# RWKV7 attention with a GELU MLP on one core: four heads of the attention's output stay in the tile in which they are made, the fifth column alone passes DRAM, and the first 430 entries of the order are new

## The chip, the cores and the metric

The kernel runs on one core of a Trainium2 chip. The core has five engines that run side by side: TensorE (PE, matmuls), VectorE (DVE), ScalarE (ACT), GpSimd (POOL) and SyncE (SP), which here does nothing but issue DMAs. The metric is the time of one execution on the device in microseconds (us); several executions are made and the median is taken.

## The reference

```python
def _attn_ref(r, k, v, w, a, b):                 # (4, 8, 768, 40) each: batch, heads, seq, head_dim
    state = np.zeros((B, H, D, D), dtype=np.float32)
    for t in range(S):
        y[:, :, t] = np.einsum('bhd,bhde->bhe', rt, state)
        Sa = np.einsum('bhde,bhe->bhd', state, at)
        state_decay = state * wt[:, :, None, :] - np.einsum('bhd,bhe->bhde', Sa, bt)
        state = state_decay + np.einsum('bhd,bhe->bhde', vt, kt)

def _moe_ref(x, w_in, w_out):                    # (3072, 320), (320, 2048), (2048, 320)
    h = x @ w_in
    g = h * (1.0 / (1.0 + np.exp(-1.702 * h)))
    return (g @ w_out).astype(np.float32)

x = np.ascontiguousarray(attn_out.transpose(0, 2, 1, 3)).reshape(B * S, H * D)
return _moe_ref(x=x, **moe_kwargs)
```

A recurrence over 768 time steps for each batch and head, and then an MLP over all 3072 tokens. All is computed in float32.

## The kernel before

**Units.** Time is cut into 12 chunks `c` of 64 steps, the batches into 2 pairs `p`. A unit is `i = 2c + p`. Inside a chunk the recurrence is turned into matrix products: decays are summed (`ps_cum`, `ps_cumc`), ScalarE takes their exponentials (`G`, `GT`, `FT`), inputs are scaled by them (`b`, `ak`, `rv`, `kh`, `bh`), a triangular 64x64 matrix `N` is made for each head and inverted in five levels (`ps_level`), right sides `B0` and `B1` are built (`ps_B`), solved (`ps_X`, `M`), and one last group of matmuls (`ps_y`, `read`) gives both the output of the chunk and the state for the next. From `ps_y`, `updated` makes the new state, `read_out` the sum of output terms, and `decayed` (L956 to L962) multiplies by the decay and so makes x, the attention's output, of the unit, with 40 channels of a head on the partitions of one half (rows 0 to 39 and 64 to 103) and heads and time along the free axis.

**The MLP** of a chunk follows both of its units. It needs x with all 320 channels along the contraction, as 5 columns `k` of 64 rows in each half (`xT`, three slots, so three chunks). Before, x goes through DRAM for that: `part_with` (L967) writes the tile x, 80 KB from each half, to a DRAM tile of 320 rows, and `get_back` (L973) reads it into both halves of `xT`, 160 KB each. An `up` task (L986) is 4 matmuls (two instructions each) for one of 4 quarters `q` of the hidden size, one `m` of 2 and one `k` of 5: 40 tasks a chunk. `gelu` (L995) is one ScalarE instruction per `q`. `down` has 8 parts for each `p`, and then two evictions and a store.

**Weights.** The 8 pieces of w_in and w_out come in four quarters each, as pairs of words, and pass four instructions (L447, L455, L459, L463) before they can be used. Their raw data lies in places that are free at the start; that of the fifth piece lies in slots 1 and 2 of `xT`, so those slots may be written only once this piece is joined.

**Order.** All work is 2700 tasks, each with the tasks that it must follow. A list, `ORDER`, names every task by number, the letter of its engine (p, a, d, g, s for PE, ScalarE, VectorE, GpSimd, SyncE) and the PSUM bank, and `Plan.listed` (L89) hands them out in that sequence: each engine runs its own entries in the order of the list, and waits where a task that it must follow is not done. SyncE issues its DMAs in this order too, with at most 8 in flight. A helper records every matmul, so all of PE's rows name line 300; they are told apart by tile.

```python
x_of = lambda: buf("x", i, [128, 4, 2, 64])
...
for e in BITS:
    nc.sync.dma_start(rows()[e], x_of()[64 * e:64 * e + D].rearrange("p j b t -> p (j b t)"))
```

Of the kernel before, what the change touches and what calls it, by code (L numbers as in the profile page):

```python
# [107 lines left out]
0s 5s 7s 8s 9s 3a 6s 87p0 88p1 24s 89a1 1s 2s 12s 102a 95d 100p2 90a0 93d 158a 101d2 98p3 96g 10s 94d 17s 97g 16s 99d3 103p1  # L108
4a 11s 132p0 104a1 105d1 142p2 26s 143p3 133a0 106d 130p1 14s 144a3 13s 107p0 15s 18s 151g 108a0 109d0 51s 131a1 110p3 27s
149g 150d 111a3 112d3 159p0 156p1 145a2 161d0 160a0 152g 113p3 345s 92a 162d 25s 153d 114a3 163p2 42s 115d3 34s 19a 274s 264p0  # L110
165d2 265p3 164a2 22d 266a3 166p2 20d 273s 21d 33s 43s 167a2 154p3 168d2 23g 35s 28a 157d1 116p2 155d3 169p1 117a2 118d2 267a0
279d 63s 280g 119p3 277s 171d1 36s 44s 120d3 343s 125d3 278g 124d3 29d 126p2 170a1 123a3 30d 172p1 122a3 127a2 121a 31d 128p2
54s 173a1 287a 288p0 289a0 129d2 32g 174d1 134p3 147s 37a 290d0 175p2 135d3 180a2 146s 178a2 275s 176d2 136p1 179a2 479s 38d
181a2 45s 39d 177a 282g 291d 91s 138a1 182p0 188p3 281d 183a0 186p2 139d 137a1 283p0 187a2 184p1 189a3 40d 276s 292p2 46a
284d0 41g 285p3 185d1 344s 148a 286d3 190p0 293a2 294d2 334p1 335p3 357a 140s 191d0 268g 336a3 315d 192p2 47d 337a1 348d 316p0
194a2 295p3 349d 61s 317a0 195g 60s 347s 358p1 296a3 62s 297d3 360d1 318a0 298p3 271a 361d 319p0 338g 300d3 196s 193a2 320a0
346s 355p2 385d 270s 48d 299a3 362p0 356d2 351g 301p3 363a0 364d0 350g 269s 141s 386p2 197s 302d3 365p0 387a2 352g 359a1 303d3
388a2 323p1 367d0 366a0 321p3 49d 324a1 304p2 322a3 478s 325d1 50g 353p0 309a2 470p3 354d0 209p1 307a2 210p1 310a2 305d2 211p1
308a2 272d 198p0 341a 199p0 72s 212p1 70s 64a 200p0 340s 368p2 52s 342d 339s 69s 201p0 369a2 202p0 370d2 203p0 471a 213p1 65d
214p1 389p2 66d 472a3 483g 204p0 390a2 560s 371p3 67d 306a 53s 215p1 71s 482s 216p1 372a3 217p1 476a 220p2 373d3 68g 218p1  # L120
221p2 477d 219a1 205p0 222p2 206p0 223p2 224p2 207p0 55a 311p3 225p2 79s 312d3 80s 226p2 208a0 58d 313p1 374p3 314d1 227p2 56d
379a3 228p2 229p2 57d 326p0 230a2 59g 393p1 327d0 378a3 391p2 394a1 375d3 231p0 558s 392d2 376a 232p0 233p0 395d1 559s 81s 73a
78s 234p0 480s 381p2 235p0 328p1 481s 382a2 74d 377a3 485d 380a3 236p0 75d 492a 242p2 486d 243p2 82a 76d 484d 77g 383p3 237p0
384d3 244p2 329d1 330d1 488p3 473d 238p0 531d 245p2 487g 246p2 489d3 85d 532p1 239p0 533a1 396p3 331d 332s 474s 475s 534a1
240p0 247p2 397d3 562s 241a0 535p1 83d 490p3 536a1 84d 398p0 572a 491d3 86g 550p1 555s 561s 253p3 399d0 551a 333s 400d0 254p3
401d 402s 554s 255p3 552a1 564d 493p0 705s 556a 567g 570p1 403s 494d0 248p2 563d 566g 249p2 495d0 498d 256p3 571d1 565g 250a2
496a0 251d2 252s 696p1 497g 557d 539p0 537p2 704s 257p3 538a2 540d0 258p3 553d 611d 697a 499d 573p2 784s 700s 259p3 576a2
574d2 710d 260p3 541d0 575d2 404p0 578d 261a3 577g 405p0 579d 698a1 568p2 711g 500p1 406p0 569d2 501a1 407p0 262d3 263s 708s
580p2 702a 502d1 408p0 582d2 409p0 503d 410p0 583d 504a 612p3 411p0 584g 613d3 412p0 614d3 413p0 505p1 709d 414a0 426p3 506d1
427p3 428p3 507d1 429p3 699d 581d2 430p3 615p1 785s 706s 701s 703d 431p3 616a1 585p0 432p3 508d 586a0 433p3 587d0 434p3 509a  # L130
588d 435p3 589d 448p2 436a3 510p1 590p0 511a1 449p2 592d0 591a0 512d1 415p3 513d 416p3 593d 514a 417p3 594g 418p3 515p0 419p3
516a0 517d0 595p1 518d 420p3 596a1 597d1 421p3 598d 422p3 519a 599d 423p3 424p3 520p0 425a3 437p1 521d0 438p1 523d0 522g 439p1
524d0 440p1 525d0 441p1 442p1 526d0 527p3 718p0 929s 528a3 443p1 719d0 787s 444p1 720d0 529p3 445p1 721d0 446p1 530d3 600p0
723d 447a1 542p3 722d 724g 603d0 605a0 619p1 604d0 543d3 450p2 620a1 606d0 544p3 621d1 601d0 602d 617p1 707s 546d3 451p2 618a1
783s 712d 547g 713d 607p0 725p1 608a0 452p2 609p0 453p2 548s 610d0 932s 454p2 727d1 726d1 622p0 728d 545d3 729a 775p1 455p2
623d0 780s 776a 549s 756d 730p3 624p0 456d2 457d2 731d3 458s 459p2 777a1 778g 732d3 786s 788g 781a 779s 626d0 460p2 625d0 627g
733d 795p1 835d 734a 461p2 735p3 791g 462p2 628s 736a3 796d1 737d3 716p0 792g 738d 463p2 782d 739g 1011s 920p1 757p3 925s
464p2 717d0 758a3 629s 759a3 790d 465p2 740p0 789d 466p2 741a0 742d0 921a 797p3 467d2 760p0 1008s 468d2 800a3 923d 652p2 469s
761d0 922a1 653p2 926a 930s 798d3 714p1 799d3 654p2 924s 802d 801g 655p2 934d 803a 656p2 836p0 657p2 715d1 658p2 659p2 837d0
762p3 838d0 927d 660p2 763a3 661p2 764p1 662a2 743d 630p0 744d 928s 631p0 632p0 765d1 804p3 766d1 633p0 805a3 806d3 634p0 807d  # L140
635p0 808a 745p2 636p0 748d2 637p0 749d2 839p1 933g 750d2 638p0 840a1 1009s 751d2 639p0 809p3 746d2 935g 640a0 641p1 810d3
642p1 793p2 747a 811d3 674p0 812d 794d2 813a 752p3 643p1 753a3 814p2 644p1 815a2 816d2 754p3 645p1 755d3 646p1 817d 647p1 818a
767p2 841p3 768d2 648p1 842a3 649p1 819p2 650p1 820a2 821d2 675p0 769p3 822d 651a1 823d 771d3 931s 770d3 772g 824p2 936d 676p0
827a2 828a2 942p1 829a2 677p0 1153s 830a2 937d 945a1 773s 663p3 825d2 664p3 943d1 1156s 826a 665p3 944d1 999p2 947d 946g 666p3
1000a 1004s 980d 940p1 948g 667p3 941d1 668p3 774s 669p3 670p3 831p1 671p3 1001a2 1002d 1003s 832d1 672p3 1005a 1013d 678p0
673a3 1006d 833p2 843p1 679p0 834d2 1007s 844d1 938p2 845d1 680p0 939d2 846p3 681p0 847d3 949p1 1012g 682d0 848p2 950a1 683d0
1014d 684s 685p3 849d2 1015g 1010s 850d2 1021p0 1016g 951d1 686p3 1024a0 1232s 851d 1235s 981p2 687p3 982a2 952d 852s 1022d0
983a2 953g 1144p1 1023d0 688p3 1026d 1145a 1149s 1025d 1027g 984p2 1059d 689p3 1154s 954p0 853s 985a2 1147g 690p3 1158d 1148s
955a0 956d0 986p2 1146a1 957d 1150a 691p3 958d 987a2 1151d 988p0 692p3 989a0 1152s 990d0 959p1 693a3 865p2 960a1 694d3 866p2
961d1 867p2 695s 962d 868p2 963d 1028p0 869p2 1029a0 1030d0 870p2 1031d 1157g 871p2 1159d 1032a 1060p3 872p2 873p2 1061a3  # L150
874p2 1062d3 1033p1 875a2 854p0 1035d1 855p0 1036d 856p0 1037d 1063p3 857p0 1064d3 1034a1 858p0 964p2 859p0 965a2 966d2 1038p1
967d 860p0 1039a1 1040d1 861p0 1041d 1017p3 968a 1042g 862p0 1018d3 863p0 969p2 864a0 876p1 970d2 877p1 972d2 971g 1043p3
973d2 878p1 1044a3 974d2 879p1 975d2 880p1 881p1 1045d3 1019p0 1046d 976p2 1047a 882p1 1020d0 1233s 883p1 977a2 1166p3 884p1
1169a3 1167d3 1377s 978p0 885p1 1168d3 898p2 1171d 1170g 886a1 979d0 887p3 1172a 1048p0 991p1 1051a0 888p3 1052a0 992d1 889p3
1053a0 890p3 1054a0 891p3 1049d0 993p1 1050a 1067p0 994d1 1160g 1155s 892p3 1161d 1068a0 893p3 894p3 1069d0 1380s 895p3 1204d
1065p0 995d1 896p3 996d 1066a0 1231s 1055p1 899p2 897a3 1056d1 997s 1173p0 1223p3 900p2 1174a0 1175d0 1228s 1176d 1224a 1177g
1057p1 901p2 1058d1 1070p0 998s 1164p1 1225a3 1226d 1236g 1227s 1071d0 902p2 1229a 1165d1 1162p3 903p2 1238d 1163d3 904p2
1237d 1178p0 1230d 905p2 1179a0 1180d0 1245p1 906a2 1181d 1072p3 1248a1 1456s 907d2 1182g 1246d1 908s 1247d1 909p0 1250d 1234s
1239g 1073d3 1251a 910p0 1240g 1074d3 1249d 1183p2 1459s 1283d 1368p1 911p0 1184a2 1075d 1373s 912p0 1185d2 1369a 1076s 1186d
1252p3 1187d 913p0 1370a1 1371g 1372s 1382d 1253a3 1188p2 1254d3 1374a 914p0 1255d 1190d2 1256g 1077s 1189a2 1191d 1243p1  # L160
1375d 915p0 1192g 1257p3 916p0 1244d1 1258a3 1259d3 1205p2 917d0 1206a2 1193p1 918d0 1207a2 1089p3 1260d 919s 1196a1 1090p3
# [87 lines left out]
def rwkv7_gelu_quick(ctx: ExitStack, tc: tile.TileContext, time_d, v_d, w_d, wc_d, ak_d, b_d, rv_d, w_in, w_out, out):  # L249
# [8 lines left out]
    NM = NF // 2  # L258
    NK = DM // 64
    NQ = NM // 2  # L260
    LEVELS = 5
# [721 lines left out]
    def mlp(c):  # L983
# [154 lines left out]
```

## Time and profile before

| | before |
|---|---|
| median of 3 runs | 678.64 us (678.22 to 679.32) |
| span of the profiled execution | 676.5 us |
| what lies around the span, against the median | 2.1 us |
| TensorE busy | 648.5 us, 96% |
| VectorE busy | 444.6 us, 66% |
| ScalarE busy | 331.6 us, 49% |
| GpSimd busy | 175.3 us, 26% |
| moved by DMA | 69.74 MB, 103 GB/s over the span |

The profile is one execution. The page gives busy times of engines and the span in 40 slices with one digit for each (9 is 90% or more). From the trace behind it come rows by stretch of time (windows), the chain of waits that ended last, and the timeline of each engine, in which a row may join several instructions (x4). "issue" means that the engine waited for nothing that the profile shows. A releaser such as `<-DMA b<-in_b` is what ended the idle time before an instruction.

### The profile page before, as it was taken

The page shows a single profiled execution, that of the slowest core. Times are in us where ns is not written, and L with a number is a line of the kernel's source. Part 1 is how long each engine was busy: PE and PEld are TensorE (multiplying, and loading weights), DVE is VectorE, ACT ScalarE, POOL GpSimd, SP SyncE. Part 2 cuts the span into 40 slices and gives each one's busy share as a digit, 9 for nine tenths or more (in the row PEclk, how much of TensorE's full clock was granted, in tenths as well). Part 3 has the DMA queues.
Part 4 walks back from the last instruction along what each step waited for, and adds up shares of the span by engine and source line. Part 5 has one row for each costly group of instructions (what it writes and reads, how often), then busy time and mean ns, then how long its engine had stood idle before and what let it go on. Part 6 is the DMA issues. An engine that isn't in the chain of part 4 may idle for free.

```text
span 676.5 us, 42217 instructions
## 1 busy us (share of the span) xinstructions
PE 648.5 (96%) x19488; PEld 553.4 (82%) x19488; DVE 444.6 (66%) x908; ACT 331.6 (49%) x710; POOL 175.3 (26%) x204
## 2 busy tenths in 40 slices
PE   5768999999999999999999999999999999999997
PEld 5657887987998987788888888798888798798785
DVE  4786787777867667767776587768656766675001
ACT  4676755534564655664545445455454354252110
POOL 6344244224123123123123211322412421300000
PEclk9899999999999999999999999999999999999999
DMA  7983736315314314432404413513412411200200
GB/s 230 300 289 94 232 107 187 103 43 154 108 47 149 93 58 117 121 108 72 118 22 132 141 34 109 156 33 108 140 39 71 122 53 54 61 14 15 61 12 20
DMA packets 35313, 69.74 MB, mean 103 GB/s; under 512 B 5440, under 2 KB 14656, under 8 KB 35136
## 3 DMA queue, kind: packets, MB, share of 16 engines
q1 hardware_dynamic: 35136, 67.03, 32.6%
q8 instruction: 153, 2.51, 1.5%
q14 instruction: 24, 0.20, 0.1%
HBM read 59.15 MB, written 7.86 MB: 99 GB/s over the span
## 4 chain that ended last, share of the span: by engine, by line
PE 93%; DMA 2%; DVE 2%; issue 1%; ACT 1%; DVEq 0%; SPq 0%; ACTq 0%
PE ps_up L300 31%; PE ps_down L300 30%; PE ps_level L300 9%; PE ps_y L300 5%; PE ps_B L300 5%; PE ps_X L300 2%; PE ps_N L300 2%; PE ps_rz L300 2%; PE ps_RV L300 2%; PE ps_A L300 2%; PE ps_zT L300 1%; DMA ak<-in_ak 1%; PE ps_cum L300 1%; PE ps_T L300 1%; DMA b<-in_b 1%
## 5 line engine op out<-in xcount | busy, mean ns | idle before, releaser
L300 PE MATMUL ps_up<-xT_all,w_sb 64*64 64x256 f32 x3840 | 251.0, 377 | 0.8 <-issue 0.4
L300 PE MATMUL ps_down<-w_sb,g 64*64 64x320 f32 x3072 | 237.0, 430 | 0.2 <-ACT zr L877 0.2
L300 PEld LDWEIGHTS ps_up<-xT_all,w_sb 64*64 64x64 f32 x3840 | 170.1, 133 | 15.9 <-issue 1.5
L300 PEld LDWEIGHTS ps_down<-w_sb,g 64*64 64x64 f32 x3072 | 128.0, 133 | 42.8 <-ACT zr L877 0.4
L996 ACT ACTIVATE g<-ps_up 128x1024 f32<-128x1024 f32 x48 | 49.2, 1024 | 45.4 <-PE ps_up L300 45.0
L715 POOL TENSOR_TENSOR EX<-ES,quads 128x512 f32<-128x512 f32 x29 | 38.3, 1322 | 112.7 <-DVE ES L708 74.9
L300 PEld LDWEIGHTS ps_level<-W,EX 64*64 64x64 f32 x2560 | 57.8, 134 | 6.7 <-DVE T L838 0.5
L758 ACT COPY W<-ps_level 128x512 f32<-128x512 f32 (+1 forms) x56 | 29.5, 527 | 67.7 <-PE ps_level L300 65.7
L760 DVE TENSOR_TENSOR E<-two,ps_level 128x256 f32<-128x256 f32 x80 | 33.1, 415 | 34.2 <-ACT W L758 30.1
L300 PE MATMUL ps_level<-W,EX 64*64 64x64 f32 (+1 forms) x2560 | 55.4, 217 | 0.1
L713 ACT ACTIVATE EX<-ES,quads 128x256 f32<-128x256 f32 x80 | 36.3, 501 | 31.0 <-DVE ES L708 30.3
L619 POOL TENSOR_TENSOR ak<-ak,FT 128x512 f32<-128x512 f32 x16 | 20.9, 1305 | 76.6 <-DMA ak<-in_ak 53.4
L708 DVE STREAM_TRANSPOSE ES<-E 128x256 f32<-128x256 f32 x80 | 35.3, 443 | 4.4
L300 PE MATMUL ps_level<-PT,EX 64*64 64x64 f32 (+2 forms) x1280 | 32.8, 235 | 5.1 <-DVE EX L729 3.7
L300 PEld LDWEIGHTS ps_level<-PT,EX 64*64 64x64 f32 x1280 | 30.8, 139 | 8.3 <-DVE EX L729 4.2
L300 PE MATMUL ps_y<-M,bh 64*64 64x104 f32 (+1 forms) x768 | 35.6, 250 | 0.7 <-DVE M L915 0.4
L300 PE MATMUL ps_y<-RV,kh 64*64 64x104 f32 (+1 forms) x768 | 35.6, 251 | 0.0
L899 ACT COPY B<-ps_B 128x416 f32<-128x416 f32 (+1 forms) x34 | 16.6, 492 | 33.4 <-PE ps_B L300 33.2
L300 PEld LDWEIGHTS ps_y<-RV,kh 64*64 64x64 f32 x768 | 28.3, 137 | 2.6 <-DVE M L915 0.5
L689 DVE COPY_PREDICATED PT<-within,ps_N 128x256 f32<-128x256 uint32 x40 | 17.8, 444 | 18.5 <-ACT P L697 13.5
L915 DVE TENSOR_TENSOR M<-ps_X,later 128x832 f32<-128x832 f32 (+1 forms) x24 | 23.8, 993 | 8.3 <-PE ps_X L300 8.1
L300 PE MATMUL ps_B<-RV,A 64*64 64x104 f32 (+1 forms) x768 | 27.9, 252 | 1.1 <-issue 1.1
(131 smaller groups left out, 1088.2 us busy)
## 6 DMA issues: line engine op xcount, KB each, us to landing
ak<-in_ak SPq DMA_DIRECT2D x48, 160.0 KB
rv<-in_rv SPq DMA_DIRECT2D x48, 160.0 KB
time<-in_time SPq DMA_DIRECT2D x24, 320.0 KB
xT_all<-x_dram SPq DMA_DIRECT2D x48, 160.0 KB
wc<-in_wc SPq DMA_DIRECT2D x20, 264.0 KB
logw<-in_w SPq DMA_DIRECT2D x24, 160.0 KB
RV<-in_v SPq DMA_DIRECT2D x24, 160.0 KB
b<-in_b SPq DMA_DIRECT2D x48, 80.0 KB
```

What stands on the lines that cost most here:

```text
L300: nc.tensor.matmul(o, lhsT, rhs, start=start, stop=True, skip_group_check=True)
L619: plan.add(R, {"DVE": 690.0, "POOL": 1270.0, "sbuf": True}, lambda t: of(t.engine).tensor_mul(ahT(), ahT(), FT_of(i)), reads=T("ak", "FT") ...
L689: plan.add(R, dve(256), lambda t, n=n: nc.vector.copy_predicated(tiles_of(at(E0_t, i)), every(within_of(n), [128, 2, 4, 32]), blocks(psum( ...
L708: plan.add(rank, dve(256), lambda t: nc.vector.transpose(ES(n), source(t)), writes=[key("ES", n, 6)], **reads)
L713: nc.scalar.activation(dst[:, :, h], ES(n), ACT.Copy, scale=quads[:, h, :1])
L715: of(t.engine).tensor_mul(dst, ES(n).unsqueeze(2).to_broadcast([128, 8, 2, 32]), quads.unsqueeze(1).to_broadcast([128, 8, 2, 32]))
L758: plan.add(rank, any2(512 - 8 * past), lambda t: copy(t.engine)(tiles_of(W(n + 1))[:, :, :, past:], blocks(psum(t, ""), 64)[:, :, :, past: ...
L760: plan.add(rank, dve(256), lambda t: nc.vector.tensor_sub(tiles_of(E(n + 1)), every(two32, [128, 2, 4, 32]), blocks(psum(t, ""), 64)[:, :, ...
L899: plan.add(R, any2(4 * wide), lambda t: copy(t.engine)(dst(), some(psum(t, "")[:, :, :208])), writes=[("Bv", i)] if x and c > 0 else T("B" ...
L915: plan.add(R + 1, dve(8 * wide), lambda t: nc.vector.tensor_tensor(M_of(i)[:, :, :wide].rearrange("p (j b) n -> p b j n", b=2), some(psum( ...
L996: plan.add(-45, {"ACT": 1030.0, "table": "gelu"}, lambda t: nc.scalar.activation(g_of(c * NQ + q).rearrange("p m r n -> p r m n"), psum(t, ...
```

## The change

The tile x is gone. `decayed` writes straight into `xT`: rows 0 to 39 of each half now hold four heads of that half's own channels, as the four columns k = 0 to 3. What is missing is the other half's share. Of the 40 rows of the far half, 24 are copied from SBUF to SBUF into rows 40 to 63 (48 KB each way), and the last 16 rows, 64 channels in each half, are written to a DRAM tile of 128 rows (32 KB from each half) and read back as column k = 4 (32 KB to each half). So `part_with` issues four DMAs instead of two, and `get_back` two, of 32 KB instead of 160. The `up` tasks of k = 0 to 3 follow the side copies (`xm`), those of k = 4 the way back (`xs`). The rows of w_in are put in the new order of channels on the host, apart for each half. The `up` loop runs k outside and m inside, so that the numbers of its tasks mean other pieces. `decayed` now must follow what `get_back` had to: the MLP tasks that last read its slot of `xT`, and for chunks 1 and 2 the fifth weight.

In `ORDER` the first 430 entries are the same tasks in a new sequence, with other banks and in part other engines: 103 of them stood on VectorE and 124 do now, ScalarE has 79 instead of 97, GpSimd 21 instead of 24, PE 123 and SyncE 83 as before. From entry 431 on the numbers and engines are the same.

```diff
-                     ..., zT=1, M=2, x=1, xT=3, g=4, ob=1), 4)
+                     ..., zT=1, M=2, xT=3, g=4, ob=1), 4)
...
-        x_of = lambda: buf("x", i, [128, 4, 2, 64])
+        x_of = lambda: xT_of(c)[:, p, :4].rearrange("p j (b t) -> p j b t", b=2)
...
-        plan.add(R + 6, {...}, decayed, reads=T("y", "FT"), uses=T("rz"), writes=T("x"))
-        rows = lambda: drams[i].rearrange("(e d j) n -> e d (j n)", e=2, d=D)
+        plan.add(R + 6, {...}, decayed,
+                 reads=T("y", "FT") + ([("weight", raws.index("x"))] if c in (1, 2) else []), uses=T("rz"), writes=T("x"), room=[("xT", c)])
 
         def part_with(t):
             if i not in drams:
-                drams[i] = dram.tile([DM, 2 * C], FP32, tag=f"x{i}", name="x_dram")
+                drams[i] = dram.tile([128, 2 * C], FP32, tag=f"x{i}", name="x_dram")
+            side = lambda lo, hi: xT_of(c)[lo:hi, p, :4].rearrange("p k n -> p (k n)")
             for e in BITS:
-                nc.sync.dma_start(rows()[e], x_of()[64 * e:64 * e + D].rearrange("p j b t -> p (j b t)"))
+                far = 64 * (1 - e)
+                nc.sync.dma_start(drams[i][HALF[e]].rearrange("(d j) n -> d (j n)", j=4), side(far + SIDE, far + D))
+            for e in BITS:
+                far = 64 * (1 - e)
+                nc.sync.dma_start(side(64 * e + D, 64 * e + 64), side(far, far + SIDE))
 
         def get_back(t):
             for h in HALF:
-                nc.sync.dma_start(xT_of(c)[h, p].rearrange("q k n -> q (k n)"), drams[i].rearrange("(q k) n -> q (k n)", q=64))
+                nc.sync.dma_start(xT_of(c)[h, p, 4], drams[i][h])
...
-            plan.add(R + q, pe((1, 256)), go, reads=[("xs", (c, p)) for p in BITS] + [("weight", q)],
+            plan.add(R + q, pe((1, 256)), go, reads=[("xs" if k == NK - 1 else "xm", (c, p)) for p in BITS] + [("weight", q)],
...
-            for m in BITS:
-                for k in range(NK):
+            for k in range(NK):
+                for m in BITS:
                     up(q, m, k)
```

The order's first line before and after:

```diff
-0s 5s 7s 8s 9s 3a 6s 87p0 88p1 24s 89a1 1s 2s 12s 102a 95d 100p2 90a0 93d 158a 101d2 98p3 96g 10s 94d 17s 97g 16s 99d3 103p1
+0s 3a 87p3 9s 1s 102a 4a 5s 6s 2s 88p0 89a0 90a3 92a 10s 24s 146s 11s 26s 27s 14s 93d 94d 103p0 96g 95d 143p1 97d 105d0
...
```

More of the change, by code (lines that the diff above doesn't have):

```diff
@@ L1105, in halves @@
         return n.reshape(*t.shape[:2], 2, 8 * 33)
[L1108 removed]
+    rows = [[[d + D * (e + 2 * j) for j in range(H // 2)] for d in range(D)] for e in range(2)]
+    side = 64 - D
+    order = []
+    for own, far in (rows, rows[::-1]):
+        last = [n for d in far[side:] for n in d]
+        order.append([[*four, last[q]] for q, four in enumerate(own + far[:side])])
     def pieces(x):
```

292 lines of the change are left out of this document (150 added, 142 removed).

## The prediction

> **What bounds the kernel now.** I read the head of the page first, then the busy time in stretches, then the chain of waits, and last the timelines of the engines round the places that the chain names.
>
> ```profile
> span 676.5 us, 42217 instructions
> PE 648.5 (96%) x19488; PEld 553.4 (82%) x19488; DVE 444.6 (66%) x908; ACT 331.6 (49%) x710; POOL 175.3 (26%) x204
> PE   5768999999999999999999999999999999999997
> PEclk9899999999999999999999999999999999999999
> DMA  7983736315314314432404413513412411200200
> ```
>
> TensorE (PE) is busy 96% of the span, and its row of slices is below 9 only in the first four slices (17 us each) and the last. The change removes no matmul. So nearly all that it can win is PE's idle time at the start. The windows put numbers on that. Their columns are the stretch, its length, busy time (instructions) of PE, PEld, DVE, ACT and POOL, the granted clock, the share of the DMA engines that is busy, and GB/s.
>
> ```profile
> 0.00:16.00 16.00, 8.85 (x236) 8.34 (x240) 8.07 (x14) 7.16 (x25) 9.67 (x42) 1.00 0.75 222
> 16.00:24.00 8.00, 6.29 (x211) 5.84 (x207) 3.79 (x6) 4.05 (x9) 3.35 (x3) 0.79 0.86 306
> 24.00:44.00 20.00, 13.09 (x527) 10.74 (x519) 18.08 (x31) 15.44 (x43) 9.34 (x5) 1.00 0.94 299
> 44.00:59.30 15.30, 11.34 (x464) 10.61 (x464) 9.79 (x18) 9.64 (x24) 7.47 (x10) 0.89 0.45 149
> 59.30:67.60 8.30, 6.75 (x300) 6.13 (x304) 5.85 (x10) 5.23 (x13) 3.08 (x2) 1.00 0.48 141
> 67.60:76.00 8.40, 7.18 (x169) 5.93 (x164) 5.92 (x8) 5.79 (x15) 1.59 (x2) 1.00 0.74 243
> 76.00:108.50 32.50, 32.50 (x932) 28.59 (x936) 27.30 (x43) 22.07 (x42) 14.22 (x7) 1.00 0.51 160
> 108.50:676.50 568.00, 562.53 (x16703) 477.25 (x16692) 365.75 (x784) 262.24 (x544) 126.59 (x136) 1.00 0.28 83
> ```
>
> The cut at 108.5 us is where PE ends the last of its tasks among the first 430 entries of the order. Both orders hold the same tasks in those 430 entries, 123 of them on PE, and the same sequence after them. Up to 108.5 us PE works 86.0 us (the first seven rows added) and idles 22.5: 21.3 before 67.6, where the first matmul of the MLP runs, 1.2 in the next row, none after that. From 76 us on the MLP's matmuls, which need nothing new, fill every hole that the attention leaves. Behind 108.5 us only 5.5 us are idle, the drain at the end among them.
>
> So the question has three parts: when does the first MLP task start, how much PE work is done by then, and how much idle time follows? This is the chain of waits before that point (start, length, what):
>
> ```profile
> 19.43 1.10 PE ps_N L300 x29
> ...
> 33.29 7.16 DMA ak<-in_ak
> ...
> 46.59 0.45 PE ps_RV L300 x29
> ...
> 48.09 2.13 issue
> ...
> 51.86 2.34 PE ps_y L300 x61
> 54.20 0.37 PE ps_zT L300 x25
> 54.56 0.97 PE ps_level L300 x40
> ...
> 61.95 0.34 PE ps_zT L300 x29
> 62.29 1.09 PE ps_level L300 x40
> ...
> 65.72 0.60 PE ps_B L300 x17
> ...
> 67.01 0.47 PE ps_A L300 x32
> ```
>
> It is unit 1's attention (N at 19.43 to y, done at 54.20), then pieces of units 2 and 3 that stand ahead of the MLP in PE's list. The first MLP task starts at 67.55.
>
> **The change, part by part.** *A. Loads.* Unit 1's chain starts when its b arrives, as VectorE's row shows:
>
> ```profile
> 18.48 0.69 DVE L621 SCALAR_TENSOR_TENSOR b<-b,GT 128x512 f32<-128x512 f32 x1 [0.22 <-DMA b<-in_b]
> ```
>
> ```profile
> extra<-in_w_in SPq DMA_DIRECT2D x8, 320.0 KB
> rv<-in_rv SPq DMA_DIRECT2D x48, 160.0 KB
> wc<-in_wc SPq DMA_DIRECT2D x20, 264.0 KB
> RV<-in_v SPq DMA_DIRECT2D x24, 160.0 KB
> ```
>
> In the new list four rv transfers (640 KB), one RV (160) and two quarters of a weight (640) stand behind that b instead of ahead of it, and one wc (264) stands ahead: 1176 KB less, 1.204 MB. At the 306 GB/s of 16 to 24 us this is 3.9 us, at the 222 of the first stretch 5.4. I take 4.0, as that b lands in the second of these stretches.
>
> *B. Unit 1's chain*, 19.43 to 54.20, is 34.8 us and keeps its tasks; one inversion level of unit 2 (0.97 us, the row at 54.56) now stands ahead of y: +1.0. VectorE gets more: up to unit 1's M, which y reads, its list holds 54 entries instead of 46, most taken from ScalarE. At the price of a PSUM copy that is 8 x 0.59 = 4.7 us:
>
> ```profile
> 88.45 0.59 DVE L899 COPY B<-ps_B 128x416 f32<-128x416 f32 x1
> ```
>
> Room for it is in the stretch that the chain spans:
>
> ```profile
> 18.48:44.00 25.52, 18.61 (x708) 16.06 (x704) 21.15 (x36) 18.23 (x48) 10.24 (x7) 0.93 0.91 297
> ```
>
> VectorE idles 4.4 us there, so by capacity 0.3 is left over; I take +0.5. The bounds are 0 (the entry leaves a ScalarE that is 71% busy and is served as soon) and 4.7 (no hole lies where it is needed). Upwards, PE's own 2.13 us of "issue" at 48.09, which no other engine explains, may fall elsewhere, and y ran 2.34 us where a later one takes 1.43, in the stretch with a granted clock of 0.89:
>
> ```profile
> 90.81 1.43 PE ps_y L300 x64
> ```
>
> I keep both in, as bounds of -2.1 and -0.9. Unit 1's y ends at 54.2 - 4.0 + 1.0 + 0.5 = 51.7.
>
> *C. From y to the first MLP task* PE took 67.55 - 54.20 = 13.35 us. Now zT of unit 3 (0.34), its first level (1.09), the B of unit 2 (0.60), and RV and A of unit 3 (0.45, 0.47) come behind that task: 2.95 us. The level of B above (0.97) is already paid. So 9.4 us are left, and the first MLP task starts at 61.1.
>
> *D. The path of x* has to be in time for that. These are SyncE's rows (start, time on the queue) and the sizes:
>
> ```profile
> 46.56 0.43 SPq L469 DMA_DIRECT2D extra<-in_w_out  x1
> 56.70 0.68 SPq L971 DMA_DIRECT2D x_dram<-x  x2
> ...
> 58.84 2.90 SPq L975 DMA_DIRECT2D xT_all<-x_dram  x4
> ```
>
> ```profile
> x_dram<-x SPq DMA_DIRECT2D x48, 80.0 KB
> xT_all<-x_dram SPq DMA_DIRECT2D x48, 160.0 KB
> ```
>
> Part_with was issued 2.5 us after y; it is now four DMAs, 4 x 0.34 = 1.4 us of issuing, of 32 and 48 KB instead of two of 80. The side copies are issued by 51.7 + 2.5 + 1.4 = 55.6. No small SBUF-to-SBUF transfer is in this trace; before, the whole return was issued by 61.7 (58.84 + 2.90) and had landed by 67.55, so at most 5.8 us. With that as landing the copies are there at 61.4 at the latest, so they are about level; a nearer row in size is not there, and I add nothing. The last column (64 partitions by 512 B) has a second trip, but is first needed 8 MLP tasks and several others later. Two more issues per unit delay nothing: SyncE issues nothing between 46.99 and 56.70. Later in the kernel the x transfers shrink from 480 KB to 224 a unit, which nobody waits for: PE idles nowhere in 76 to 108.5. The Trainium skill, DMA: Bandwidth & Descriptors, section Rules for kernel authors, speaks against this part: under 64 KB a transfer is mostly overhead, so four of 32 and 48 KB should gain little over two of 80 KB. By its figure of about 2 us for the fixed part (same page, anatomy of one DMA) an estimate has the side copies there at 57.6, ahead of need; this trace has no such transfer to test it.
>
> *E. The new waits of `decayed`.* It now writes into xT itself. Of chunks 1 and 2 it must wait until the fifth weight, whose raw data lies there, is joined, and behind it VectorE's list would stand still:
>
> ```profile
> 86.34 2.99 POOL L463 TENSOR_TENSOR w_sb<-w_sb,xT_all 128x1280 int32<-128x1280 int32 x1 [5.50 <-DVE w_sb L455]
> 99.84 0.89 DVE L961 TENSOR_TENSOR x<-zr,FT 128x128 f32<-128x128 f32 x4
> ```
>
> The weight is done at 89.3, unit 2's `decayed` starts at 99.8: 10.5 us of margin, so nothing. From chunk 3 on it waits for the MLP tasks of three chunks earlier, which PE's list has two chunks ahead (a chunk is about 676.5 / 12 = 56 us): nothing.
>
> *The sum.* Of PE's 46.3 us of work before 67.6 (five rows), 2.95 move behind the first MLP task, so 86.0 - 43.4 = 42.6 us follow it. Idle time after it: the rows 59.3 to 76 idle 1.55 + 1.22 of 16.7 us, 16.6%. From 61.1 to 76 that makes 2.5 us, and 0.5 for VectorE's fuller list (it idles 5.2 us in 76 to 108.5, and PE none). The set then ends at 61.1 + 42.6 + 3.0 = 106.7 instead of 108.5: 1.8 us less. What follows is the same, so the span is 674.7. The median of the runs, 678.64, is 2.1 above the profiled span, so I forecast 676.8.
>
> **The rivals.** *R1, slower: VectorE becomes the bound of unit 1.* All 4.7 us come through, because the holes of 18.5 to 44 lie at its start while the row 24 to 44 has VectorE busy 18.08 of 20. Then the first MLP task starts at 65.3, the set ends at 65.3 + 42.6 + 3.0 = 110.9, 2.4 later: 681.0. It is slower than before as soon as 2.3 of the 4.7 come through. For it: the 18.08. Against it: ScalarE, 15.44 of 20 in that row, is relieved of the same entries, and unit 1 enters the stretch 4 us earlier.
>
> *R2, no change: one more window at half clock.* The clock rows are 0.79 of 8 us and 0.89 of 15.3: 1.7 us lost in each. The Trainium skill, TensorE: Matmul & The Clock Gate, Part 1: The HAM clock gate, says that the gate is either full or half and is decided in free-running windows of about 3.4 us, idle ones bringing the half rate; the two rows agree with one half-rate window each. A new order moves the idle spots against these windows. One window more gives 676.8 + 1.7 = 678.5.
>
> *R3, a bigger gain: the 2.13 us of issue and the slow y (0.9) both go,* as y runs 2.5 us earlier: 673.8.
>
> *R4, the change does not do what it says: x's trip was hidden, and is no shorter.* If a small copy takes as long as the ak transfer in the chain, 7.16 us, side copies land at 55.6 + 7.2 = 62.8, the first MLP task waits 1.7 us, and 678.5 is left: what loads and order gain, x gives back. Against it: ak went when the DMA engines were 94% busy, these at 45 to 48%.
>
> **How the numbers follow.** About 0.2%, 1.4 us, can be told from no change. The forecast 0.37 and R3 0.11 are faster; R2 0.15 and R4 0.09 are within; R1 0.28 is slower. Faster 0.48, same 0.24, slower 0.28. The likeliest is 676.8. Its own bounds: minus 3.0 (R3's terms), plus 1.7 (half clock): 673.8 to 678.5. To hold 8 in 10 the range must take in most of R1 as well: 673.5 to 681.1, which leaves out the worse half of R1 and a little beyond R3.
>
> **What would show each step right or wrong.** In the profile of the changed kernel: A, VectorE's b of unit 1 at about 14.5; B, its y ends near 51.7, and VectorE's busy share in 24 to 44 stays under 0.95; C, the first MLP task near 61; D, no PE wait for a side copy or the returned column in the list of waits; the sum, PE idle about 3 us from there to the end of the set, near 106.7, and every row after it shifted by the same amount. Wrong would be a b that comes no earlier (other loads filled its place), a y at 55 or later with VectorE as releaser (R1), a third clock row clearly under 1 (R2), or idle time of 5 us and more behind the first MLP task.

## The result: 680.99 us against 678.4, slower by 0.45%

| | before | changed |
|---|---|---|
| median of 20 runs each, one chip | 678.4 us (674.41 to 680.75) | 680.99 us (678.72 to 683.25) |
| ratio of the runs | | 1.0045, 95% interval 1.0032 to 1.0058 |
| span of the profiled execution | 676.5 us | 679.1 us (its time 681.0) |

The forecast was 676.8, a gain of 1.8 us; the time lies inside its range, on the other side of no change. One execution differs from the next by 1.2 to 2.8 us (the standard deviation of a kernel's runs), so sizes below are differences of means with their 95% interval, always against runs on the same chip. Comparisons leave out runs that took over 1.5% longer than the fastest of their kernel; only the short kernels that stop early had such runs. Over the four sets of runs that the changed kernel got (56 runs on four occasions) the difference is +2.2 us, plus or minus 0.5.

The head of the page of the changed kernel shows much the same picture as before: PE is below 9 in the first slices, and VectorE's first slices are fuller (6888, where the kernel before has 4786):

```profile
span 679.1 us, 42282 instructions
PE 651.8 (96%) x19488; PEld 548.5 (81%) x19488; DVE 456.6 (67%) x936; ACT 322.3 (47%) x684; POOL 173.3 (26%) x201
PE   5787989999999999999999999999999999999997
DVE  6888979777867667767776587867656766675001
PEclk9987999999999999999999999999999999999999
```

The windows of the changed kernel, at the cuts of the prediction (columns as there), and then at its own milestones: y of unit 1 ends at 51.3, the first MLP task starts at 63.98, PE ends the first 430 entries at 109.73.

```profile
24.00:44.00 20.00, 14.82 (x537) 13.23 (x535) 17.66 (x32) 10.20 (x29) 7.28 (x7) 0.83 0.58 184
44.00:59.30 15.30, 10.31 (x411) 9.10 (x404) 13.39 (x22) 7.17 (x18) 8.22 (x6) 0.88 0.57 183
59.30:67.60 8.30, 8.10 (x237) 7.65 (x234) 5.61 (x11) 5.04 (x11) 3.14 (x1) 0.80 0.79 235
76.00:108.50 32.50, 30.15 (x936) 23.74 (x932) 28.17 (x46) 15.40 (x31) 13.80 (x6) 1.00 0.65 202
...
51.30:63.98 12.68, 8.99 (x297) 8.59 (x301) 11.46 (x20) 6.67 (x15) 4.55 (x5) 0.73 0.65 209
63.98:76.00 12.02, 11.76 (x310) 9.28 (x306) 9.85 (x20) 9.36 (x12) 5.72 (x2) 1.00 0.64 217
109.73:679.10 569.37, 563.10 (x16704) 473.27 (x16696) 367.18 (x785) 262.66 (x546) 127.05 (x137) 1.00 0.26 73
```

Two things stand out. Between y and the first MLP task VectorE is busy 11.46 of 12.68 us, 90%. The same stretch of the kernel before, cut at its own milestones, had it busy 65%, and its clock column reads 1.00:

```profile
54.20:67.55 13.35, 10.51 (x504) 9.61 (x498) 8.62 (x14) 9.17 (x20) 7.35 (x9) 1.00 0.39 115
```

And from 76 to 108.5 PE, which never stopped there before, idles 2.35 us. The list of PE's waits from 60 to 112 us names for whom (the columns: tile, what it waited for, us in total, times, longest):

```profile
PE ps_X L308 <- DVE B L910: 1.5, 1, 1.5
PE ps_A L308 <- DVE Tc L813: 0.5, 1, 0.5
PE ps_T L308 <- DVE M L923: 0.4, 1, 0.4
```

VectorE's and GpSimd's timelines at that place show how VectorE came to be late:

```profile
94.82 1.70 DVE L627 TENSOR_TENSOR ak<-ak,FT 128x512 f32<-128x512 f32 x1
96.44 2.23 DVE L969 TENSOR_TENSOR xT_all<-zr,FT 128x128 f32<-128x128 f32 x4
98.60 0.58 DVE L907 COPY B<-ps_B 128x416 f32<-128x416 f32 x1
99.21 0.59 DVE L910 TENSOR_TENSOR B<-ps_B,B 128x416 f32<-128x416 f32 x1
...
93.00 2.97 POOL L471 TENSOR_TENSOR w_sb<-w_sb,extra 128x1280 int32<-128x1280 int32 x1 [5.27 <-DVE extra L467]
96.16 1.08 POOL L635 TENSOR_TENSOR bh<-time,G 128x320 f32<-128x320 f32 x1 [0.20 <-DMA time<-in_time]
97.21 0.91 POOL L635 TENSOR_TENSOR kh<-time,G 128x320 f32<-128x320 f32 x1
```

Unit 4's ak takes 1.70 us where the same instruction takes 0.68 elsewhere (at 12.04, say), and `decayed` 2.23 where the prediction's row had 0.89. Each began while GpSimd was in an instruction of its own, and the two evictions of B, for which PE's X waits, stand behind both. The Trainium skill, SBUF — State Buffer, section Who interferes with whom, says that a VectorE instruction with two SBUF inputs contends with a GpSimd instruction that reads SBUF, and that the ports they share are an exclusive lock. The rows agree: GpSimd's join ends at 95.97, and 0.68 after that is 96.65, where the ak in fact ends at 96.52.

Between y and the first MLP task the same is seen on a smaller scale. This is the chain of waits there (start, length, what), with three VectorE rows and three GpSimd rows of that time behind it:

```profile
51.37 1.28 DVE ak L627
52.64 1.08 DVE zr L861
53.72 0.14 issue
53.86 0.50 PE ps_zT L308 x28
...
57.19 0.91 issue
...
59.00 1.74 PE ps_level L308 x38
```

```profile
51.37 1.28 DVE L627 TENSOR_TENSOR ak<-ak,FT 128x512 f32<-128x512 f32 x1
52.57 1.14 DVE L861 TENSOR_TENSOR zr<-zraw,wz 128x320 f32<-128x320 f32 x1
53.63 1.76 DVE L629 SCALAR_TENSOR_TENSOR b<-b,GT 128x512 f32<-128x512 f32 x1
...
51.24 0.86 POOL L635 TENSOR_TENSOR kh<-time,G 128x320 f32<-128x320 f32 x1 [1.04 <-PE ps_y L308]
52.06 1.31 POOL L635 TENSOR_TENSOR bh<-time,G 128x320 f32<-128x320 f32 x1
53.32 1.52 POOL L632 TENSOR_TENSOR ak<-ak,GT 128x512 f32<-128x512 f32 x1
```

PE's next entry was unit 2's zT, and PE waited 2.58 us for zr. What zr reads had been made by 41.7, but in VectorE's list it stood behind a transpose, which waited for ScalarE and PE, and behind ak. Then the clock halved: a level that took 0.97 took 1.74, and the clock column reads 0.73 for the whole stretch.

This is one execution. Three more profiles of the changed kernel were taken beside the experiments. In this stretch PE waits for zr in each of them, 2.6, 1.6 and 1.3 us. Its own "issue" waits there are 0.9 us in the first profile and 1.7, 2.8 and 3.1 in the others, and the clock columns read 0.73, 1.00, 0.86 and 0.86. Two rows of the third profile's waits from 16 to 112 us:

```profile
PE ps_rz L308 <- issue: 3.5, 2, 2.8
PE ps_zT L308 <- DVE zr L861: 1.6, 1, 1.6
```

### The profile page after: what moved, and what is told of

Its sections match the earlier page's. It is cut to its first block, busy times and chain, and to the rows that moved or that the text cites. A ratio compares the mean times of both kernels' runs of the same rounds, so it can differ in the third digit from the quotient of the medians.

```text
span 679.1 us, 42282 instructions
## 1 busy us (share of the span) xinstructions
PE 651.8 (96%) x19488; PEld 548.5 (81%) x19488; DVE 456.6 (67%) x936; ACT 322.3 (47%) x684; POOL 173.3 (26%) x201
## 4 chain that ended last, share of the span: by engine, by line
PE 91%; DVE 5%; issue 1%; DMA 1%; ACT 1%; SPq 1%; DVEq 0%; ACTq 0%
PE ps_up L308 30%; PE ps_down L308 30%; PE ps_level L308 10%; PE ps_B L308 4%; PE ps_y L308 4%; PE ps_X L308 2%; PE ps_N L308 2%; PE ps_A L308 2%; PE ps_RV L308 2%; PE ps_rz L308 2%; PE ps_zT L308 1%; DVE EX L737 1%; PE ps_T L308 1%; PE ps_Q L308 1%; PE ps_cum L308 1%
## 5 line engine op out<-in xcount | busy, mean ns | idle before, releaser
L308 PE MATMUL ps_up<-xT_all,w_sb 64*64 64x256 f32 x3840 | 246.6, 377 | 0.6 <-issue 0.2
L308 PEld LDWEIGHTS ps_up<-xT_all,w_sb 64*64 64x64 f32 x3840 | 161.6, 133 | 21.5 <-DVE B L910 0.7
L308 PEld LDWEIGHTS ps_level<-PT,EX 64*64 64x64 f32 x1280 | 32.6, 147 | 7.2 <-DVE EX L737 2.2
L627 POOL TENSOR_TENSOR ak<-ak,FT 128x512 f32<-128x512 f32 x14 | 18.3, 1310 | 75.6 <-DMA ak<-in_ak 47.5
L308 PE MATMUL ps_level<-PT,EX 64*64 64x64 f32 (+2 forms) x1280 | 35.2, 246 | 2.5 <-DVE EX L737 1.2
L308 PE MATMUL ps_y<-M,bh 64*64 64x104 f32 (+1 forms) x768 | 34.2, 246 | 0.0
L907 ACT COPY B<-ps_B 128x416 f32<-128x416 f32 (+1 forms) x31 | 15.1, 488 | 37.2 <-PE ps_B L308 37.0
L635 POOL TENSOR_TENSOR kh<-time,G 128x320 f32<-128x320 f32 x20 | 17.4, 870 | 54.6 <-PE ps_y L308 35.3
```

Of the source, the lines that this page charges most:

```text
L308: nc.tensor.matmul(o, lhsT, rhs, start=start, stop=True, skip_group_check=True)
L627: plan.add(R, {"DVE": 690.0, "POOL": 1270.0, "sbuf": True}, lambda t: of(t.engine).tensor_mul(ahT(), ahT(), FT_of(i)), reads=T("ak", "FT") ...
L635: plan.add(R + 4, {"POOL": 870.0, "DVE": 490.0, "sbuf": True}, lambda t, n=n, dst=dst: of(t.engine).tensor_mul(dst(i)[:, :, :D], by_head(t ...
L907: plan.add(R, any2(4 * wide), lambda t: copy(t.engine)(dst(), some(psum(t, "")[:, :, :208])), writes=[("Bv", i)] if x and c > 0 else T("B" ...
```

## The experiments

All edits are to the list or to a few lines. The milestones of the profiled executions, to which the text keeps coming back (us; "rest" is from the end of the 430 entries to the end of the span):

| profile of | y of unit 1 ends | first MLP task | 430 entries end | rest |
|---|---|---|---|---|
| before | 54.2 | 67.6 | 108.5 | 568.1 |
| new way of x, old order (twice) | 51.1, 52.2 | 67.9, 68.6 | 107.7, 108.0 | 571.6, 567.5 |
| forecast | 51.7 | 61.1 | 106.7 | 568.0 |
| changed (four times) | 51.3, 52.8, 50.9, 51.2 | 64.0, 64.6, 63.4, 63.6 | 109.7, 110.5, 109.5, 110.8 | 569.4, 570.0, 566.7, 568.1 |
| new order, old way of x | 49.9 | 61.2 | 109.2 | 570.1 |
| five entries moved (twice) | 48.9, 51.5 | 59.5, 62.2 | 105.8, 106.3 | 567.7, 568.8 |
| six entries moved (twice) | 50.3, 50.3 | 60.4, 60.8 | 107.4, 107.0 | 566.9, 570.5 |

The rest scatters over 5 us without regard to the kernel; the front is what the change moves.

**The way of x alone, and the order alone.** The changed kernel with the whole old list:

```diff
-ORDER = """0s 3a 87p3 9s 1s 102a ...        (new list)
+ORDER = """0s 5s 7s 8s 9s 3a 6s ...         (old list, the same task numbers)
```

> The path of x alone: the changed kernel with the old order of all 2700 entries (the same task numbers; the k-outer up loop and the four DMAs of the way of x stay). If the loss lies in the new order of the first 430 entries, this runs at the time of the kernel before, 678.4, or a little under, since 256 KB fewer move per unit and PE waits for none of it: 677.5 to 679. If the four small DMAs cost the time (a side copy is issued in 0.8 us instead of 0.34), it is slower by most of the 2.6 to 3 us: 680.5 to 681.5, with the first MLP task later than 67.6.

The kernel before with the new list, and a second buffer for x so that unit 3's product may be listed ahead of unit 2's DMA:

```diff
-M=2, x=1, xT=3
+M=2, x=2, xT=3
-ORDER = """0s 5s 7s ...
+ORDER = """0s 3a 87p3 ...
```

> The new order alone: the kernel before with all entries of the new order; the tile x gets two buffers, since unit 3's product is listed ahead of the DMA that reads unit 2's. x goes the old way through DRAM, 480 KB a unit. If the order is what costs, it is as slow as the changed kernel: 680.5 to 682.5, with unit 1's y ending near 51 and the first MLP task at 64 or later. If the new path of x costs, the order gains what was forecast and this is near 676.5 to 677.5.

Measured on one chip: the way of x alone 681.05 us, ratio to the kernel before 1.0006 (0.9983 to 1.0029); the order alone 682.85, 1.0031 (1.0002 to 1.006). The difference between the two, 1.6 us plus or minus 1.8, is not clear on this chip. A repeat put the way of x beside the changed kernel:

> The new way of x with the old order, beside the changed kernel on one chip. Theory: level with the kernel before (within 0.8 us), so 1 to 3 us under the changed kernel: the loss is the order's. Rival: half of the loss is the way of x, and it is 1 us or more over the kernel before.

> The changed kernel as the base of the two others on this chip: 1 to 3 us over the kernel before.

Measured: the way of x alone 678.49, 0.9983 (0.9965 to 1.0001); the changed kernel 682.10, 1.0035 (1.0013 to 1.0057). The difference between these two, which have all in common but the list, is 3.8 us, plus or minus 1.4. Over both occasions the way of x moves the time by -0.6 plus or minus 0.8 (+0.4 on one chip, -1.3 on the other). So the loss is the order's. The windows of the repeat (cut at its own milestones) show PE without a hole from 76 us on, as in the kernel before:

```profile
52.23:68.60 16.37, 12.94 (x503) 12.28 (x495) 8.84 (x16) 9.47 (x22) 5.99 (x9) 0.79 0.27 78
68.60:76.00 7.40, 7.32 (x183) 5.82 (x178) 5.50 (x8) 5.91 (x16) 2.80 (x2) 1.00 0.73 244
76.00:108.02 32.02, 32.02 (x918) 27.17 (x913) 28.08 (x43) 22.03 (x42) 13.23 (x6) 1.00 0.52 161
```

The profile of the order alone is the counterpart: no half clock at all, a first MLP task at 61.2, as forecast, and yet the 430 entries end at 109.2. Its waits of PE from 60 to 112 us:

```profile
PE ps_B L301 <- issue: 1.9, 1, 1.9
PE ps_level L301 <- issue: 1.7, 1, 1.7
PE ps_X L301 <- DVE B L903: 1.6, 1, 1.6
```

The VectorE wait for B is there again, as in all profiles of the changed kernel; it belongs to the list. The two "issue" waits are PE's own. They are the larger part here, and one profile can't say how much of this kernel's loss they are.

**The front alone.** Four kernels stop after the first 540 entries and leave the rest of the output unwritten:

```diff
-    for t in tasks:
+    for t in tasks[:540]:
```

> The kernel before, cut after the first 540 entries of its list (the new order's 430 and 110 more, which are alike in both; the rest of the outputs stays unwritten). In the profiles PE ends its last task of these 540 at 132.4 us. It is the base for the three other cut kernels: the time of the front alone, without the 545 us behind it. About 134 to 137 us.

> The changed kernel cut at the same place (PE's last task ended at 133.8 us in its profile, 1.4 later than before). If the whole loss of about 3 us of the full runs comes from the first 430 entries, this is 2.5 to 3.5 us over the cut kernel before. If the new way of x, or the noise of the long rest, carries half of it, it is 1 to 1.7 us over. If the front is no slower in the middle of many runs, the loss lies behind it.

> The new way of x with the old order, cut at the same place. In its full profile PE ended the first 430 entries 0.7 us before the kernel before. Theory: it changes nothing in front, within 0.7 us of the cut kernel before. Rival: the slower side copies (0.8 us each to issue) delay loads behind them on SyncE, and it is 1 us or more slower.

> The new order with the old way of x, cut at the same place. Theory: the order alone makes the front slower, by VectorE's waits at 76 to 110 us and by half-clock windows or issue stalls ahead of that: 1 to 3 us over the cut kernel before, like the changed kernel cut. Rival: order and way of x only cost together, and this is within 0.7 us of the cut kernel before.

Measured: before 134.6 to 135.1 us (3 of 6 runs), changed 137.7 to 139.0 (4), the order alone 136.7 to 138.1 (4), the way of x alone one run only, 136.1. In parts of the kernel before's whole time: 0.1985 (0.1978 to 0.1992), 0.2036 (0.2027 to 0.2045), 0.2022 (0.2014 to 0.203). This points to the front, and to the order, but weakly. The medians of all six runs are 136.8 for the kernel before, 138.7 for the changed one, 137.9 for the order alone and 138.5 for the way of x alone, with runs of one kernel up to 7 us apart. So the sizes are rough, and the way of x is not decided here.

**All entries back on their old engines,** the new sequence kept:

```diff
-... 289d ... 394d ... 483d ...      (39 entries on other engines than before)
+... 289a ... 394a ... 483g ...
```

> The changed kernel with the sequence of its list kept, but every entry back on the engine on which it stood before (23 from VectorE to ScalarE, 7 from VectorE to GpSimd, 5 and 4 to VectorE). If VectorE's fuller list delays the work between unit 1's y and the first MLP task, VectorE is relieved of about 12 us and the set gains 2 to 4 us: 677 to 679. If the sequence itself is at fault (which task stands behind which), nothing is gained: 680.5 to 682, or worse, as the sequence was made for the other engines.

Measured: 691.39 us, 1.0156 (1.0113 to 1.0199), ten us worse than the kernel before, against my theory that relief of VectorE as such would help. In its waits from 16 to 112 us PE now waits for GpSimd and ScalarE as well as for VectorE:

```profile
PE ps_N L302 <- POOL ak L621: 4.2, 1, 4.2
PE ps_level L302 <- ACT PT L794: 3.3, 3, 2.3
PE ps_X L302 <- DVE T L840: 2.5, 1, 2.5
```

So less work on VectorE is not enough; the new sequence needs the new engines. That what counts is which entry stands in front of which is tested further down.

**Keeping PE busy in the wait for zr.** Matmuls that nobody reads, in a free half of zT's bank:

```diff
                 ps = psum(t, "ps_zT")
+                if i == 2:
+                    for n in range(6):
+                        for e, f in QUARTERS:
+                            mm(ps[HALF[f], e, 256:512], ident[HALF[e]], starts[HALF[e]].rearrange("p j t -> p (j t)")[:, :256], True)
```

> The changed kernel with 24 matmuls of 64x64 on 64x256 that nobody reads (24 x 0.108 = 2.6 us, from the 0.4325 us of an up task of four) put ahead of unit 2's zT, in the 2.6 us in which PE waits for VectorE's zr there; the results are the same. If the two half-clock windows from about 55.8 to 62.6 us come from that idle stretch, they go, the granted clock of 51.3 to 64 rises from 0.73 to 0.9 or more, and the time falls by 2 to 3 us: 678 to 679. If VectorE is the bound there anyway and the slower PE is hidden, the clock rises and the time stays at 680.5 to 681.5. If the windows don't hang on this idle time, neither changes, or the time rises by what the matmuls delay zT.

Measured: 686.68 us, 1.008 (1.0052 to 1.0109). In the profile the half clock is gone (1.00 throughout), the first MLP task starts at 60.2 and the 430 entries end at 107.2, 1.3 ahead of the kernel before: which is what the theory of the clock asked of the front. But the order alone had no half clock either and ended its front at 109.2, and here GpSimd's join ended at 92.87, before ak (0.68 us) began, so that the wait for B is missing too: this one execution doesn't say which of the two it was. The rest took 574.3 us, where it otherwise took 566.7 to 571.6. PE is idle 2.93 us between 110 and 670 there, mostly "issue", and 0.67 in the kernel before (0.6 to 2.4 in the profiles of the other lists):

```profile
110.00:670.00 560.00, 557.07 (x16536) 492.89 (x16532) 366.06 (x778) 262.33 (x544) 127.48 (x137) 1.00 0.26 73
```

```profile
110.00:670.00 560.00, 559.33 (x16612) 475.14 (x16608) 363.44 (x780) 262.24 (x544) 125.09 (x135) 1.00 0.28 83
```

Why a few dozen instructions at 50 us slow the next 570 is open. As a test of what the half clock costs the whole kernel, this run is inconclusive.

The granted clock of each run says more, because it is on record for all of them. On the three chips of its repeats the changed kernel's mean clock was 0.9934, 0.9936 and 0.9931, against 0.9919, 0.9922 and 0.9910, and yet it was slower by 1.2, 1.9 and 2.5 us. On the last of these chips the way of x alone, 3.8 us faster, had 0.9908. The kernel that kept PE busy had 0.9950 against 0.9917, and was 5.5 us slower. So half-clock time is not what makes the changed kernel slower over its runs; if anything it had less.

**Moving VectorE's entries.** One edit behind the first MLP task, one ahead of it, and both; the changed kernel ran beside them.

```diff
 late:  -  483d 331d ... 394d 395d ... 485d 397d
        +  ... 394d 395d 483d 331d ... 397d 485d      (B of unit 3 ahead of ak and decayed)
 early: -  191d ... 297d 348d 315d                    (zr of unit 2 behind a transpose that waits for PE)
        +  191d 315d ... 297d 348d
        -  183a ... 289d
        +  183a 289a                                  (P of unit 2 to ScalarE, where it is idle)
```

> The changed kernel once more, so that the three others have it on the same chip: about 0.45% over the kernel before, 681 to 683. Its profile should again show VectorE's unit 4 ak and unit 2 decayed at about 1.7 and 2.2 us instead of 0.68 and 0.89, beside GpSimd's join of a weight, and PE idle for 2 to 3 us between 76 and 110, where the kernel before idles 0.

> The changed kernel with three entries of VectorE's list moved: unit 4's ak and unit 2's decayed behind the two evictions of unit 3's B, and the second ak behind unit 3's M. Theory: the idle time of PE in 76 to 110 is VectorE's B coming late, since these two run into GpSimd's join and take 1.0 and 1.3 us longer; now B is evicted first, PE's wait of 1.5 us for it goes, idle in 76 to 110 falls from 2.3 to 3.2 to under 1.2, and the time falls by 1 to 2 us against the changed kernel on the same chip. Rival: the loss is PE's instruction stalls and half-clock windows, and the time does not move by more than 0.5.

> The changed kernel with two entries moved ahead of the first MLP task: unit 2's zr straight behind unit 1's M on VectorE (it was ready and stood behind an instruction that waited for PE), and unit 2's two P on ScalarE, which was idle when they were ready. Theory: PE's waits for them (2.6 us for zr, 1.0 for P in the profile) go, the first MLP task starts 1 to 3 us earlier (61 to 62), and the time falls by 1 to 2 us against the changed kernel. Rival: the following work is late anyway, and the time stays within 0.7.

> Both together. Theory: 2 to 4 us under the changed kernel, that is 677.5 to 680 where it runs at 681 to 682, and so level with the kernel before or up to 1.5 us under it, as the forecast of the change had it. Rival: under 1 us.

Measured on one chip, 12 runs each: changed 678.98 us, ratio to the kernel before 1.0013 (0.999 to 1.0036); late 679.25, 1.0012 (0.9991 to 1.0032); early 678.11, 0.9999 (0.9977 to 1.002); both 677.28, 0.9988 (0.9965 to 1.0012). Against the changed kernel that is 0.0 plus or minus 1.2, -0.6 plus or minus 1.3, and -1.2 plus or minus 1.6. The late edit did to the trace what it was made for. Its VectorE rows, and PE's idle time in 76 to 106, 0.64 us against 1.98 in the changed kernel beside it:

```profile
97.83 0.59 DVE L901 COPY B<-ps_B 128x416 f32<-128x416 f32 x1 [1.72 <-PE ps_B L302]
98.45 0.59 DVE L904 TENSOR_TENSOR B<-ps_B,B 128x416 f32<-128x416 f32 x1
98.96 0.68 DVE L621 TENSOR_TENSOR ak<-ak,FT 128x512 f32<-128x512 f32 x1
...
76.00:106.00 30.00, 29.36 (x876) 24.70 (x872) 24.78 (x41) 17.62 (x33) 11.76 (x6) 1.00 0.62 199
```

```profile
76.00:106.00 30.00, 28.02 (x846) 21.79 (x837) 25.00 (x39) 16.20 (x32) 11.39 (x6) 1.00 0.62 192
```

The wait went and the time did not move: the runs leave at most 1.2 us for the late wait, and the theory had 1 to 2. In that execution two "issue" waits, 3.9 us ahead of the first MLP task and 2.2 behind it, took what the edit gave; over the 12 runs, why nothing is left stays open. One more entry was then moved, since PE still waited 1.2 us at 54.6 us for a transpose behind `decayed` and P:

```diff
-  298p 358p 195d ... 359d ... 300d
+  298p 300d 358p 195d ... 359d
```

> The changed kernel a third time, as the base of the two others on their chip: 0.1 to 0.45% over the kernel before. In its profile PE idles 1.9 to 3.2 us between 76 and 110 us.

> The list with five entries moved, once more. Theory (VectorE's waits are the loss): 1 to 3 us under the changed kernel on the same chip, and 0 to 1.5 us under the kernel before. Rival (stalls and clock windows alone): within 0.7 us of the changed kernel.

> The same list with a sixth entry moved: VectorE's transpose of unit 2's third level stands ahead of unit 1's decayed and unit 3's P, since PE waited 1.2 us for it at 54.6. Theory: up to 1 us under the list with five moved; the wait for it goes from the list of PE's waits. Rival: unit 1's side copies and unit 3's level come later by as much, and nothing is gained.

Measured on one chip: changed 679.48, 1.0032 (1.0011 to 1.0054); five moved 677.98, 1.0008 (0.9985 to 1.0031); six moved 676.69, 0.9995 (0.9978 to 1.0012). And once more beside the changed kernel at 682.10:

> The list with six entries of VectorE and ScalarE moved, once more. Theory: 1.5 to 3.5 us under the changed kernel and 0 to 2 us under the kernel before. Rival (chance on one chip): within 1 us of the changed kernel.

Measured: 679.18, 0.9999 (0.9975 to 1.0022). Over two chips the six moved entries are worth 2.8 us, plus or minus 1.0, against the changed kernel; the five are worth 1.2 plus or minus 1.1. Against the kernel before, the six give -0.7 plus or minus 0.8: no difference that these runs can tell, and none against the way of x alone (+1.0 plus or minus 1.6 on the one chip that had both). No version was shown to beat the kernel before. The windows of the six moved (its first profile, own milestones) have the stretch from y to the first MLP task at 10.05 us instead of 12.68:

```profile
50.34:60.39 10.05, 7.90 (x288) 7.41 (x280) 9.47 (x18) 6.79 (x14) 4.05 (x5) 0.83 0.67 220
60.39:76.00 15.61, 14.63 (x398) 11.65 (x394) 12.79 (x24) 11.67 (x17) 6.09 (x2) 1.00 0.76 244
76.00:107.36 31.36, 29.04 (x879) 23.63 (x875) 26.24 (x46) 14.37 (x31) 13.56 (x6) 1.00 0.66 200
```

VectorE is still busy 94% of the first stretch and PE still idles 2.3 us in the last. PE's idle time in the first stretch is 2.2 us (2.6 in the second profile) where the four profiles of the changed kernel have 3.7 to 4.8, and its busy time, 7.9 us, lies among theirs (7.0 to 9.0). Added up over 50 to 112 us, PE's waits for VectorE are 1.2 to 1.5 us in the three profiles with the old order, 3.4 to 5.0 in the changed kernel, 2.8 and 1.3 with five entries moved, 1.2 and 1.5 with six. Its "issue" waits are 2.4 to 4.7, 0.9 to 4.5, 1.9 and 3.3, 2.8 and 2.7, in which no kernel stands out. The one profile of the order alone doesn't fit: 2.6 for VectorE and 6.8 of "issue". The gain is that the same entries, all but one on the same engine, stand in an order in which PE needs them. Which of the six does how much was not shown: neither the late nor the early edit alone was clear of the noise.

## Why the prediction was wrong, by its own steps

- **A, the loads: right in direction, under-sized.** VectorE's b of unit 1 ran at 12.64, not 14.5: 5.8 us earlier instead of 4.0 (4.6 to 6.0 in the repeats).
- **B, unit 1's chain: right in the number, partly by luck.** y ended at 51.28 (51.7 forecast; 50.9 to 52.8 in the repeats), and VectorE was busy 88% of 24 to 44, below the 95% that would have spoken for R1. But b came 1.8 us earlier than forecast and y only 0.4: from b to y took 38.6 us (38.1 to 38.9 in the repeats), where the step had 37.2, and the two errors cancel. The longer chain fits the half clock of 0.83 in that row; it wasn't tested.
- **C, from y to the first MLP task: the step that failed.** It took PE's 13.35 us, subtracted the PE work that moves behind, and got 9.4. The four profiles of the changed kernel have 12.7, 11.8, 12.5 and 12.5, so it was 2.4 to 3.3 us short. The 9.4 were 6.6 of work at full clock and, carried over unchanged from the old order, the old row's 2.8 of idle time. Measured were 7.0 to 9.0 of work, with half-clock time in three of the four, and 3.7 to 4.8 idle, of which 1.3 to 2.6 are the wait for VectorE's zr and 0.9 to 3.1 PE's own "issue". The step costed PE's list and never VectorE's, though zr waited in VectorE's list while PE needed it. With six entries in a better place the stretch is 10.05 and 10.5, of which 2.2 and 2.6 are idle.
- **D, the way of x: right that it delays nothing, late in its times.** PE's list of waits has no side copy and no returned column in it, and with the old order the new way of x costs nothing that these runs can tell (-0.6 plus or minus 0.8). So R4 falls. With six entries moved the side copies were all issued by 57.79 and the first MLP task began at 60.39 without a wait for them, so they landed within 2.6 us, not 5.8 or 7.2. What the Trainium skill's rule on small transfers (DMA: Bandwidth & Descriptors, Rules for kernel authors) had against this part, that it should gain little, agrees with the -0.6. The estimate of 57.6 had them 2 us from issue to landing, by a figure that stands on that page for DMAs that GpSimd issues; these are issued by SyncE, and no run here measures more than the bound. Two side copies take 1.60 us to issue where I put 0.34 each, and since `decayed` was late on VectorE the last was issued at 59.38, not 55.6. Had the first MLP task come at 61.1, this could have mattered; at 63.98 it didn't.
- **E, the waits of `decayed`: right,** none is seen.
- **The sum: behind the first MLP task about right, for the wrong reason.** From the first MLP task to the end of the 430 entries it had 45.6 us; the profiles have 45.7 to 47.2. But I had the idle time before 76 us, 2.5, and 0.5 for VectorE behind it, and it was the other way round: 0.26 idle from 63.98 to 76, and 2.35 behind 76, where VectorE's late B and the rest of its list stop PE. The row from which I took the 0.5, VectorE busy 84% with PE never waiting, said nothing about another sequence of the same load. Over the whole front the sum had 86.0 us of work and 20.7 idle; the four profiles have 86.6 to 88.8 and 21.0 to 23.8.
- **The rest of the kernel** was taken as unchanged, and its order is; in single executions it scatters from 566.7 to 571.6 us, so that the 2.6 us between the two profiled spans is 1.3 of front and 1.3 of scatter. Over the repeats the front is 2.0 us later than with the old order (110.1 against 108.1 on average), as the 2.2 of the times is.
- **The rivals.** R1 named VectorE, and gave 681.0; its place was wrong, and that the number fits is luck. The 4.7 us of more work were to come through before unit 1's M, and did not; PE's waits for VectorE came behind y. R2 took place in the profile: the clock columns lose 3.4, 1.8 and 1.7 us in three rows, four half-clock windows where there were two. But how many there are changes from execution to execution, none in the profile of the order alone, and over the runs the changed kernel's mean clock is not the lower one. So R2 is not what separates the two kernels. R3, a bigger gain, is out with the time.

The forecast's front, 106.7, is where the two mended lists come out (105.8 to 107.4). It described the change with a VectorE list that serves PE in time, which the list that was measured does not. Even so the time with six entries moved is 0.7 us below the kernel before, plus or minus 0.8, and so not the 1.8 of the forecast; where the difference goes is not shown.

## What to carry to other kernels

When work is moved ahead on the engine that sets the end, walk the lists of the engines that feed it through the same stretch, and not only its own. Idle time read from the old order is no evidence for a new one, and neither is a share of busy time: VectorE was 90% busy where PE waited for it and 94% busy where the mended list no longer made it wait for zr. Look for the instruction that is ready and stands behind one that isn't. And where a single execution scatters by as much as the change is worth, put the milestones of several profiles, and the granted clocks of all runs, side by side before a cause is named.

## What the runs showed of the hardware

A VectorE instruction with two SBUF inputs took longer beside a GpSimd instruction that reads SBUF. In six profiles of full kernels with this stretch of the new list, ak began inside GpSimd's join and took 1.70 or 1.71 us instead of 0.68, and `decayed` took 2.23 to 2.27 instead of 0.89 in five of them (1.55 in one). In a seventh, the kernel that kept PE busy, the join had ended 0.6 us earlier, and the two took 0.68 and 0.89. With five entries moved they ran beside no GpSimd instruction and took 0.68 and 0.89 or 0.90 again. It goes the other way too: with the late edit GpSimd's kh, beside ak and `decayed`, took 1.38 instead of 0.91.

Half-clock time in the changed kernel's first profile lasted from 31.9 to 38.7 and from 55.8 to 62.6 us (the clock reads 0.50 inside). In the 3.4 us ahead of each, PE was busy 1.40 and 1.70 us, so it had not been idle all of that time. In its other profiles such episodes lasted 3.4 us (58.7 to 62.1 in the third, say) or about twice that.

PE's waits that nothing in the trace explains, up to 3.9 us at a time, fall elsewhere in each execution. Runs of one kernel, whose instructions are fixed, had standard deviations of 1.2 to 2.8 us; what makes that scatter was not shown.
